# A DiT block on one core: other PSUM banks for the first fc1 groups, the scale rows in one block, the last x tile's transposes one K group earlier

## The chip, the cores and the metric

The kernel runs on one core of one Trainium2 chip. The time is the device time of one execution in microseconds. The compared times are medians of several executions of the same program; the profile is that of one more execution, which has a time of its own. Lower is better.

## What is computed

One diffusion transformer block on x of 2 x 256 tokens with D = 1152, in bfloat16. Cut to what matters here:

```python
mod = (silu(c) @ w_mod).reshape(B, 6, 1, D)
shift_a, scale_a, gate_a, shift_m, scale_m, gate_m = [mod[:, i] for i in range(6)]
h = layernorm(x) * (1 + scale_a) + shift_a
q, k, v = split(h @ wqkv)                    # 2 heads of 576
a = softmax(q @ k.T * 576 ** -0.5) @ v @ wo
x = x + gate_a * a
h2 = layernorm(x) * (1 + scale_m) + shift_m
return x + gate_m * (gelu(h2 @ w_fc1) @ w_fc2)   # F = 4608
```

All weights (some 50 MB) come from device memory once and pass through the core's on-chip memory.

## The kernel before, in words

**Order of the work.** Nothing loops on the chip: the Python code lists every instruction and a small planner (`Sched`) fixes its place on its engine. TensorE (PE) and the DMA queue of SyncE (SP) keep the order in which the code names the work. For VectorE (DVE), ScalarE (ACT) and GpSimd (POOL) the planner picks, by a table of assumed costs, the ready piece with the longest chain behind it, except that `S.first` (L944) writes the first pieces of DVE and ACT out by hand. Every instruction waits, on its engine, for the semaphores of exactly the instructions and transfers that it depends on; on PSUM the unit of dependence is a whole bank (L258 to L279): PE may not write a bank until all readers of what stood there are done.

**The K stage.** The 512 tokens are four x tiles of 128 tokens, `X[:, t, :]`; tiles 0 and 1 are image b = 0, tiles 2 and 3 are b = 1. Each tile is normalised: tiles 1 and 3 take mean and variance from DVE's `bn_stats` (`ln_stats_dve`, L738), tiles 0 and 2 from two accumulating passes on ACT (`ln_stats_act`, L747); POOL raises the variance to the power -1/2 (L745, L754) and DVE then writes `xn` with one `tensor_scalar` over 1152 columns (L763, pieces `xn_0` to `xn_3`). PE transposes the tile with nine 128-wide matmuls (`xn_T`, L773, recorded at L696); `hk` (L812) multiplies 256 columns by the row of 1 + scale_a and so makes K's operand `HK`, on DVE (L819) or ACT (L817).

K itself is `k_pair(kts, i, b)` (L831): two output groups of 128 columns, each a 256-wide matmul per 128 rows kt of the weights. K's weights come kt by kt. For b = 0 the loop L865 goes over kt = 0 to 4 with four pairs each (eight matmuls a kt), with tile 2's transposes behind kt = 1; of kt = 4 it does two pairs, then come tile 3's transposes (`xn_T(3)`, L870), then the other two pairs. Then `k_pair((0, 2, 1, 4, 3), 0, 1)` begins b = 1, which needs `hk_*_1`, and so tile 3's transposes.

**The scale rows.** The first five groups of 128 columns of 1 + scale_a are made early (`mod_kt`, `sc1a(0, 5)`, L860). Columns of groups 5 to 8 come as rows: `quad_mm` (L801) issues, for one kt, four matmuls of 128 columns into the four 32-column parts of the array, into bank 7. L879 does this for kt = 0 to 5 ("scb_0") behind the first K pair of b = 1, L883 for kt = 6 to 8 ("scb_1") behind `k_pair((0, 2, 1), 1, 1)`. A DVE transpose (L888) and `sc1a_5` (L890) follow, then `hk` for kt = 5 to 8. The weights `WSC` for these columns arrive in three transfers (kt 0 to 2, 3 to 5, 6 to 8: `ld_sc5_0`, `ld_sc5_3`, `ld_sc5_6`, issued at L706), behind those that are needed earlier and ahead of K's weights for kt = 5 to 8. The loads of `WQ` (L897) go to the same memory, so each waits on SP until PE has read that kt of `WSC`.

**The fc1 stage.** `xn2_T(t)` (L1142) transposes a tile of the second layer norm into two banks (7 and 6 for even t, 1 and 0 for odd t: groups 0 to 3 in the first, 4 to 8 in the second), and 9 instructions per tile, on DVE (L1154) and ACT (L1157), carry them to `H2T`. `fc1_tile(f, tok0, ntok)` (L1160) makes one group of 128 hidden columns in the next bank of the list `acc`. The first nine groups are made for tokens 0 to 255 first; tile 3's transposes (L1223) stand two groups ahead of their end. Then L1228 to L1230 put two banks, 0 and 1, ahead of the four in use, and L1231 makes the nine groups for tokens 256 to 511, which need tile 3.

Of the kernel before, what the change touches and what calls it, by code (L numbers as in the profile page):

```python
# [493 lines left out]
ALU = mybir.AluOpType  # L494
ACTF = mybir.ActivationFunctionType
# [5 lines left out]
KT = 9  # L501
# [8 lines left out]
KC = 5  # L510
# [5 lines left out]
def c_mm(n):  # L516
    return max(n / 2.4 + 2.5, 27.0)
# [14 lines left out]
def c_dve_fast(n):  # L532
    return 160.0 + 0.37 * n
# [10 lines left out]
def build_kernel(nc, x, c, wqkv, wo, w_mod, w_fc1, w_fc2, out):  # L544
    S = Sched()
# [4 lines left out]
    with (  # L550
# [4 lines left out]
        def sb(off, nbytes, dt=BF16):  # L555
            assert off % 4 == 0 and off + nbytes <= ARENA_BYTES, (off, nbytes)
            v = arena[:, off // 2:(off + nbytes) // 2]
            if dt == F32:
                v = v.bitcast(F32)
            return v  # L560

        def ps32(bank, c0=0, n=512):
            return psum[:, bank * 512 + c0: bank * 512 + c0 + n]
# [19 lines left out]
        def misc(nbytes):  # L583
            o = mo[0]
            mo[0] += (nbytes + 3) // 4 * 4
            assert mo[0] <= ARENA_BYTES
            return o

        def wmat(o, f):
            return sb(o, KT * f * 2).rearrange("p (k f) -> p k f", k=KT)  # L590

        WSC = wmat(O_A, D)
# [58 lines left out]
        NMR = sb(misc(16), 16, F32)  # L651
# [25 lines left out]
        def dve(cost, fn, reads, writes, name):  # L677
            return S.op("dve", cost, fn, reads=reads, writes=writes, name=name)

        def act(cost, fn, reads, writes, name):  # L680
            return S.op("act", cost, fn, reads=reads, writes=writes, name=name)
# [4 lines left out]
        def copy_on(eng, dst, src, n, psum16, name):  # L686
            if eng == "act":
                act(c_act(n), lambda e: e.activation(out=dst, in_=src, func=ACTF.Copy), [src], [dst], name)  # L688
            else:
                dve(c_dve_psum16(n) if psum16 else c_dve_psum32(n), lambda e: e.tensor_copy(dst, src), [src], [dst], name)  # L690

        def mm(o, l, r, st, sp, **kw):
            S.instr(lambda e: e.matmul(o, lhsT=l, rhs=r, start=st, stop=sp, **kw), reads=[l, r], writes=[o])  # L693
# [44 lines left out]
        def ln_stats_dve(src, chunks, bn_t, mv_t, rstd_t, tag):  # L738
            for ci in range(NCH):
                s, o = chunks[ci], bn_t[:, ci * 6:(ci + 1) * 6]  # L740
                dve(550, lambda e, s=s, o=o: e.bn_stats(out=o, in_=s), [s], [o], "bn_%s_%d" % (tag, ci))  # L741
            dve(210, lambda e: e.bn_aggr(out=mv_t, in_=bn_t), [bn_t], [mv_t], "aggr_" + tag)
            var = mv_t[:, 1:2]
            dve(140, lambda e: e.tensor_scalar(out=var, in0=var, scalar1=EPS, scalar2=None, op0=ALU.add), [var], [var], "veps_" + tag)  # L744
            pool(650, lambda e: e.tensor_tensor(out=rstd_t, in0=var, in1=NHALF, op=ALU.pow), [var, NHALF], [rstd_t], "rstd_" + tag)  # L745

        def ln_stats_act(src, junk, mv_t, msq, rstd_t, tag):  # L747
            mean, var = mv_t[:, 0:1], mv_t[:, 1:2]
            act(1420, lambda e: e.activation(out=junk, in_=src, func=ACTF.Square, scale=D ** -0.5, accum_out=msq), [src], [junk, msq], "sq_" + tag)  # L749
            act(1420, lambda e: e.activation(out=junk, in_=src, func=ACTF.Identity, scale=1.0 / D, accum_out=mean), [src], [junk, mean], "sum_" + tag)  # L750
            dve(170, lambda e: e.scalar_tensor_tensor(out=var, in0=mean, scalar=mean, in1=msq, op0=ALU.mult, op1=ALU.subtract),  # L751
                [mean, msq], [var], "nvar_" + tag)
            dve(150, lambda e: e.tensor_scalar(out=var, in0=var, scalar1=-1.0, scalar2=EPS, op0=ALU.mult, op1=ALU.add), [var], [var], "veps_" + tag)  # L753
            pool(650, lambda e: e.tensor_tensor(out=rstd_t, in0=var, in1=NHALF, op=ALU.pow), [var, NHALF], [rstd_t], "rstd_" + tag)  # L754

        for t in range(4):
            xt, xn, mv, rs = X[:, t, :], XN[:, t, :], MV[:, t, :], RSTD[:, t:t + 1]
            if t % 2 == 1:
                ln_stats_dve(xt, [X[:, t, i * CH:(i + 1) * CH] for i in range(NCH)], BN[:, t, :], mv, rs, "ln1_%d" % t)
            else:  # L760
                ln_stats_act(xt, xn, mv, SUMS[:, t:t + 1], rs, "ln1_%d" % t)
            m = MV[:, t, 0:1]
            dve(c_dve_fast(D), lambda e, xt=xt, xn=xn, m=m, rs=rs: e.tensor_scalar(out=xn, in0=xt, scalar1=m, scalar2=rs,  # L763
                                                                                 op0=ALU.subtract, op1=ALU.mult),
                [xt, m, rs], [xn], "xn_%d" % t)
# [7 lines left out]
        def xn_T(t):  # L773
            b = t // 2
            S.unit("pe", KT * c_mm(128), "xnT_%d" % t)
            for kt in range(KT):
                bank, c0 = xt_ps(b, kt)
                tr(ps16(bank, c0 + (t % 2) * 128, 128), XN[:, t, kt * 128:(kt + 1) * 128], IDENT)
# [19 lines left out]
        def quads(w, g0, g1, q):  # L798
            return w.rearrange("p (g q c) -> p g q c", q=4, c=32)[:, g0:g1, q, :]

        def quad_mm(bank, w, g0, g1, kt):  # L801
            n = 32 * (g1 - g0)
            for q in range(4):
                o = psum[32 * q:32 * q + 2, bank * 512:bank * 512 + n].rearrange("p (g c) -> p g c", c=32)
                mm(o, ST[:, kt:18:9], quads(w, g0, g1, q), kt == 0, kt == KT - 1, tile_position=(0, 32 * q))
# [16 lines left out]
        def k_mm(kts, j, b, bank, half):  # L822

            for kt in kts:
                mm(ps32(bank, half * 256, 256), WK[:, kt, j * 128:(j + 1) * 128], HK[:, kt, b * 256:(b + 1) * 256], kt == 0 and half == 0,
                   kt == KT - 1, skip_group_check=True)
# [4 lines left out]
        def k_pair(kts, i, b, bank=None):  # L831
            S.unit("pe", 2 * len(kts) * c_mm(256), "k%d_%d_%d" % (b, i, kts[0]))
            bank = KB[b][i] if bank is None else bank
            if kts[0] == 0:
                for kt in kts:
                    for half in range(2):
                        k_mm((kt,), 2 * i + half, b, bank, half)
            else:
                for half in range(2):
                    k_mm(kts, 2 * i + half, b, bank, half)  # L840
            if kts[-1] == KT - 1:
                eng = "act" if ev_rr[0] % 2 == 0 else "dve"
                ev_rr[0] += 1
                copy_on(eng, QK[:, 9 + 2 * i:11 + 2 * i, b * 256:(b + 1) * 256], ps32(bank).rearrange("p (j t) -> p j t", j=2), 512, False,
                        "k_ev%d_%d" % (b, i))
# [17 lines left out]
        xn_T_copy(0, (8,), "act")  # L863
        xn_T_copy(0, (5, 6, 7), "act")
        for kt in range(KC):  # L865
            for i in range(2 if kt == KC - 1 else 4):
                k_pair((kt,), i, 0)
            if kt == 1:
                xn_T(2)
        xn_T(3)  # L870
        k_pair((KC - 1,), 2, 0)
        k_pair((KC - 1,), 3, 0)
        xn_T_copy(1, (8,), "act")
        xn_T_copy(1, (5, 7), "act")
        xn_T_copy(1, (6,), "dve")
        for kt in range(KC):
            hk(kt, 1, "act" if kt % 2 else "dve")
        k_pair((0, 2, 1, 4, 3), 0, 1)
        S.unit("pe", 6 * 4 * 27.0, "scb_0")  # L879
        for kt in range(6):  # L880
            quad_mm(7, WSC[:, kt, :], KC, KT, kt)
        k_pair((0, 2, 1), 1, 1)
        S.unit("pe", 3 * 4 * 27.0, "scb_1")  # L883
        for kt in range(6, KT):
            quad_mm(7, WSC[:, kt, :], KC, KT, kt)
        n = 32 * (KT - KC)
        sct, scr = ps32(7, 0, n), MT[:, 0:n]
# [42 lines left out]
        for kt in range(KT):  # L930
            for b in range(2):
# [5 lines left out]
                else:  # L937
# [5 lines left out]

        S.first = {  # L944
# [5 lines left out]
        }  # L950

# [160 lines left out]
        acc = [2, 3, 4, 5]  # L1112
# [113 lines left out]
        dma(WFC2[:, 27:36, :], wfc2_v[:, 27:36, :], 9 * P * D * 2, "ld_wfc2_3", run=2304)  # L1226
        mlp_gate(last_h2T[0])
        k = acc_rr[0] % 4  # L1228
        acc[:] = [0, 1] + acc[k:] + acc[:k]
        acc_rr[0] = 0  # L1230
        for f in range(F0):  # L1231
            fc1_tile(f, 256, 256)
# [79 lines left out]
```

## Time and profile before

| | before |
|---|---|
| median of 3 executions | 244.43 us (244.30 to 244.53) |
| the profiled execution | 244.33 us |
| its span, first to last instruction | 242.6 us |
| mean granted TensorE clock | 1.0 |

The span is 1.7 us shorter than the profiled execution's time; the rest lies ahead of the first and behind the last instruction. In the views, a timeline row gives start, length, engine, line, operation, operands and count, and in brackets how long the engine had been idle and what ended that. PE is the matmul, PEld the load of the stationary operand, which runs beside the matmul before; SPq is a DMA being issued. The length of a matmul covers its way through the array, so that matmuls overlap: the step from start to start is what counts. A row of DMA issues ends with the time from issue to landing.

### The profile page before, as it was taken

The numbers are of one execution on the slowest core, as the hardware profiler recorded it, in microseconds if no ns is written. First come the engines' busy times: TensorE is split into PE (matmuls) and PEld (weight loads), VectorE is DVE, ScalarE is ACT, GpSimd is POOL, SyncE is SP. The second block draws the span as 40 slices with busy tenths as digits, with TensorE's granted clock in tenths as the row PEclk, the third lists the DMA queues.
The fourth block names the chain that finished last, engine by engine and source line by source line (L and its number), as shares of the span: only waits on it lengthen the run. The fifth ranks groups of instructions, "written<-read, shape, count | busy, mean of one in ns | idle before, by whom it ended". The sixth has DMA issues, their size and how long they took to land.

```text
span 242.6 us, 3964 instructions
## 1 busy us (share of the span) xinstructions
PE 237.5 (98%) x1700; PEld 145.0 (60%) x1700; DVE 116.2 (48%) x227; ACT 67.0 (28%) x138; POOL 22.4 (9%) x40
## 2 busy tenths in 40 slices
PE   7899999999999999999999999999999999999995
PEld 2588844466657656888644444444566566566564
DVE  2663447988983599669999600000022222111112
ACT  4820340436424206973233322222000000000000
POOL 1300000000023186400000110000000000000000
PEclk9999999999999999999999999999999999999999
DMA  6999999999996999969953499100000000000000
GB/s 220 378 372 390 391 387 385 404 415 406 389 353 195 357 393 392 392 188 399 351 165 83 163 317 369 44 0 3 0 16 19 16 16 16 19 16 16 21 28 19
DMA packets 30299, 51.58 MB, mean 213 GB/s; under 512 B 1611, under 2 KB 16971, under 8 KB 30283
## 3 DMA queue, kind: packets, MB, share of 16 engines
q1 hardware_dynamic: 29600, 50.14, 57.7%
q0 software_dynamic: 512, 1.19, 1.5%
q8 instruction: 13, 0.21, 0.4%
q10 hardware_dynamic: 171, 0.01, 0.0%
q14 instruction: 3, 0.02, 0.0%
HBM read 50.15 MB, written 1.19 MB: 212 GB/s over the span
## 4 chain that ended last, share of the span: by engine, by line
PE 95%; DMA 2%; ACT 1%; DVE 1%; issue 0%
PE psum L693 93%; PE psum L696 2%; DMA arena<-in_x_dram 2%; ACT arena L750 1%; ACT arena L749 0%; DVE arena L763 0%; DVE arena L819 0%; DVE arena L1254 0%; DVE arena L1255 0%; DVE arena L751 0%; DVE arena L809 0%; DVE arena L753 0%; ACT arena L733 0%
## 5 line engine op out<-in xcount | busy, mean ns | idle before, releaser
L693 PE MATMUL psum<-arena 128*128 128x384 bf16 (+8 forms) x1611 | 234.1, 314 | 2.2 <-POOL arena L719 1.5
L693 PEld LDWEIGHTS psum<-arena 128*128 128x128 bf16 (+2 forms) x1611 | 139.7, 97 | 92.2 <-issue 3.6
L1254 DVE TENSOR_TENSOR arena<-psum,arena 128x384 f32<-128x384 f32 (+2 forms) x13 | 6.8, 526 | 88.8 <-PE psum L693 88.8
L1167 ACT ACTIVATE arena<-psum 128x512 bf16<-128x512 f32 (+1 forms) x45 | 22.8, 511 | 42.4 <-PE psum L693 42.4
L688 ACT ACTIVATE arena<-psum 128x512 bf16<-128x512 f32 (+6 forms) x37 | 18.7, 534 | 36.2 <-PE psum L693 35.9
L1067 DVE SCALAR_TENSOR_TENSOR arena<-arena 128x1152 f32<-128x1152 bf16 x16 | 21.3, 1411 | 0.0
L1038 DVE SCALAR_TENSOR_TENSOR arena<-arena 128x896 f32<-128x896 bf16 x16 | 17.7, 1142 | 0.0
L690 DVE CAST arena<-psum 128x512 bf16<-128x512 f32 (+1 forms) x12 | 7.7, 646 | 10.0 <-PE psum L693 9.9
L674 POOL DMA_DIRECT2D dit_scratch<-arena x6 | 3.6, 605 | 92.9 <-ACT arena L688 53.6
L1133 POOL TENSOR_TENSOR arena<-arena 128x384 f32<-128x384 f32 x12 | 10.9, 911 | 10.7 <-DVE arena L1132 8.8
L741 DVE BATCH_NORM_STATS2 arena<-arena 128x6 f32<-128x384 f32 (+1 forms) x18 | 9.5, 549 | 4.2 <-DMA arena<-in_x_dram 3.5
L1138 ACT ACTIVATE arena<-arena 128x1152 bf16<-128x1152 f32 x4 | 5.4, 1344 | 9.7 <-DVE arena L1137 9.7
L1132 DVE TENSOR_TENSOR arena<-psum,arena 128x384 f32<-128x384 f32 x12 | 6.5, 546 | 2.8 <-DMA arena<-dit_scratch 2.0
L696 PE MATMUL psum<-arena 128*128 128x128 bf16 (+1 forms) x89 | 7.1, 219 | 0.4 <-DMA arena<-in_c_dram 0.3
L696 PEld LDWEIGHTS psum<-arena 128*128 128x128 bf16 (+1 forms) x89 | 5.8, 98 | 2.8 <-DMA arena<-in_c_dram 1.2
L1255 DVE TENSOR_TENSOR arena<-arena 128x384 bf16<-128x384 f32 (+2 forms) x13 | 6.9, 527 | 0.5
L1157 ACT ACTIVATE arena<-psum,arena 128x128 bf16<-128x128 bf16 x16 | 6.1, 455 | 2.9 <-PE psum L696 2.1
L1154 DVE TENSOR_SCALAR arena<-psum,arena 128x128 bf16<-128x128 bf16 x20 | 5.5, 335 | 2.9 <-PE psum L696 2.9
L982 ACT ACTIVATE arena<-psum,arena 128x256 bf16<-128x256 f32 x8 | 3.7, 469 | 0.4 <-DVE arena L979 0.3
L745 POOL TENSOR_TENSOR arena<-arena 128x1 f32<-128x1 f32 x6 | 3.3, 553 | 4.9 <-DVE arena L744 4.9
L935 ACT ACTIVATE arena<-arena 128x256 bf16<-128x256 bf16 x6 | 2.5, 495 | 3.3 <-DVE arena L929 3.3
L978 DVE TENSOR_REDUCE arena<-psum 128x2 f32<-128x512 f32 x4 | 2.7, 687 | 0.9 <-PE psum L693 0.9
(57 smaller groups left out, 52.5 us busy)
## 6 DMA issues: line engine op xcount, KB each, us to landing
arena<-in_w_fc_dram SPq DMA_DIRECT2D x9, 1152.0 KB, 6.9
arena<-in_w_fc_dram SPq DMA_DIRECT2D x4, 2592.0 KB, 18.2
arena<-in_w_mod_dram SPq DMA_DIRECT2D x3, 1920.0 KB, 19.6
arena<-in_wqkv_dram SPq DMA_DIRECT2D x18, 288.0 KB, 10.5
arena<-in_w_mod_dram SPq DMA_DIRECT2D x3, 864.0 KB, 13.2
arena<-in_wqkv_dram SPq DMA_DIRECT2D x1, 2592.0 KB, 16.7
arena<-in_wo_dram SPq DMA_DIRECT2D x1, 2592.0 KB, 26.1
arena<-in_w_mod_dram SPq DMA_DIRECT2D x1, 2592.0 KB, 17.6
```

Of the source, the lines that this page charges most:

```text
L688: act(c_act(n), lambda e: e.activation(out=dst, in_=src, func=ACTF.Copy), [src], [dst], name)
L690: dve(c_dve_psum16(n) if psum16 else c_dve_psum32(n), lambda e: e.tensor_copy(dst, src), [src], [dst], name)
L693: S.instr(lambda e: e.matmul(o, lhsT=l, rhs=r, start=st, stop=sp, **kw), reads=[l, r], writes=[o])
L696: S.instr(lambda e: e.transpose(o, i_, idn), reads=[i_, idn], writes=[o])
L741: dve(550, lambda e, s=s, o=o: e.bn_stats(out=o, in_=s), [s], [o], "bn_%s_%d" % (tag, ci))
L1038: dve(150 + FG * 1.1, lambda e, o=o, w=w, s1=s1: e.scalar_tensor_tensor(out=o, in0=w, scalar=s1, in1=o, op0=ALU.mult, op1=ALU.add), [w, s1 ...
L1067: u = dve(1300, lambda e, o=o, w=w, s1=s1: e.scalar_tensor_tensor(out=o, in0=w, scalar=s1, in1=o, op0=ALU.mult, op1=ALU.add), [w, s1, o], ...
L1132: dve(550, lambda e, o=o, ga=ga, x1c=x1c: e.tensor_tensor(out=x1c, in0=o, in1=ga, op=ALU.mult), [o, ga], [x1c], "wo_t1_%d_%d" % (t, ci))
L1133: S.op("pool", 930, lambda e, xs=xs, x1c=x1c: e.tensor_tensor(out=x1c, in0=x1c, in1=xs, op=ALU.add), reads=[x1c, xs], writes=[x1c], name=" ...
L1167: act(c_act(ntok), lambda e: e.activation(out=dst, in_=o, func=ACTF.Gelu_apprx_tanh), [o], [dst], "gelu_%d_%d" % (f, tok0))
L1254: dve(c_dve_psum32(w), lambda e, o=o, gm=gm, t1=t1: e.tensor_tensor(out=t1, in0=o, in1=gm, op=ALU.mult), [o, gm], [t1], "fc2_t1_%d_%d" % ( ...
L1255: dve(c_dve_32(w), lambda e, t1=t1, x1c=x1c, ost=ost: e.tensor_tensor(out=ost, in0=t1, in1=x1c, op=ALU.add), [t1, x1c], [ost], "fc2_out_%d ...
```

## The change

1. Tile 2 is normalised on ACT: DVE makes `-mean * rstd` in one small instruction (`nmr_2`), ACT writes `xn_2` with one activation over 1152 columns. In the orders written by hand `nmr_2` stands ahead of `sc1a_0` on DVE, `xn_2` leaves DVE's list and stands ahead of `hk_4_0` on ACT.
2. Of kt = 4 one pair instead of two goes ahead of tile 3's transposes, three instead of two behind.
3. The scale rows of kt = 0 to 8 are one block, where kt = 6 to 8 stood.
4. The first two of the fc1 groups for tokens 256 to 511 use banks 6 and 7 instead of 0 and 1.

```diff
             m = MV[:, t, 0:1]
+            if t == 2:
+                nm = NMR[:, t:t + 1]
+                dve(170, lambda e, nm=nm, m=m, rs=rs: e.scalar_tensor_tensor(out=nm, in0=m, scalar=-1.0, in1=rs, op0=ALU.mult, op1=ALU.mult),
+                    [m, rs], [nm], "nmr_%d" % t)
+                act(1344, lambda e, xt=xt, xn=xn, nm=nm, rs=rs: e.activation(out=xn, in_=xt, func=ACTF.Identity, scale=rs, bias=nm),
+                    [xt, rs, nm], [xn], "xn_%d" % t)
+                continue
...
         for kt in range(KC):
-            for i in range(2 if kt == KC - 1 else 4):
+            for i in range(1 if kt == KC - 1 else 4):
                 k_pair((kt,), i, 0)
             if kt == 1:
                 xn_T(2)
         xn_T(3)
-        k_pair((KC - 1,), 2, 0)
-        k_pair((KC - 1,), 3, 0)
+        for i in range(1, 4):
+            k_pair((KC - 1,), i, 0)
...
         k_pair((0, 2, 1, 4, 3), 0, 1)
-        S.unit("pe", 6 * 4 * 27.0, "scb_0")
-        for kt in range(6):
-            quad_mm(7, WSC[:, kt, :], KC, KT, kt)
         k_pair((0, 2, 1), 1, 1)
-        S.unit("pe", 3 * 4 * 27.0, "scb_1")
-        for kt in range(6, KT):
+        S.unit("pe", KT * 4 * 27.0, "scb")
+        for kt in range(KT):
             quad_mm(7, WSC[:, kt, :], KC, KT, kt)
...
-                    "xn_1", "xn_0", "nvar_ln1_2", "veps_ln1_2", "xnT_cp0_0", "sc1a_0", "hk_0_0", "hk_1_0", "hk_2_0", "hk_3_0", "xn_2",
+                    "xn_1", "xn_0", "nvar_ln1_2", "veps_ln1_2", "xnT_cp0_0", "nmr_2", "sc1a_0", "hk_0_0", "hk_1_0", "hk_2_0", "hk_3_0",
...
-            "act": ["touch", "ld_c", "sq_ln1_0", "c_tanh", "sum_ln1_0", "sq_ln1_2", "sum_ln1_2", "xnT_cp0_8", "xnT_cp0_5", "hk_4_0",
+            "act": ["touch", "ld_c", "sq_ln1_0", "c_tanh", "sum_ln1_0", "sq_ln1_2", "sum_ln1_2", "xnT_cp0_8", "xnT_cp0_5", "xn_2", "hk_4_0",
...
-        acc[:] = [0, 1] + acc[k:] + acc[:k]
+        acc[:] = [6, 7] + acc[k:] + acc[:k]
```

## Prediction

> **What bounds the kernel now.** The page first: how busy is the busiest engine, and does anything other than its own work set the end?
>
> ```profile
> PE 237.5 (98%) x1700; PEld 145.0 (60%) x1700; DVE 116.2 (48%) x227; ACT 67.0 (28%) x138; POOL 22.4 (9%) x40
> ```
>
> PE is busy for 237.5 us, 98% of the span. Its busy time hides short stalls, because a matmul's recorded length covers its way through the array. So the second view is the timeline of PE and PEld in the two places that the change touches, where I compare starts with counts. First the K stage, from tile 2's transposes (L696) to the end of the scale rows (128*2):
>
> ```profile
> 13.32 0.67 PE L696 MATMUL psum<-arena 128*128 128x128 bf16 x9
> 13.83 2.35 PE L693 MATMUL psum<-arena 128*128 128x256 bf16 x20
> 16.01 0.67 PE L696 MATMUL psum<-arena 128*128 128x128 bf16 x9
> 16.51 0.60 PE L693 MATMUL psum<-arena 128*128 128x256 bf16 x4
> ...
> 17.12 1.03 PEld L693 LDWEIGHTS psum<-arena 128*128 128x128 bf16 x10 [0.29 <-DVE arena L819]
> 18.36 0.08 PEld L693 LDWEIGHTS psum<-arena 128*2 128x2 bf16 x1 [0.21 <-issue]
> 18.79 0.10 PEld L693 LDWEIGHTS psum<-arena 128*128 128x128 bf16 x1
> 19.55 0.10 PEld L693 LDWEIGHTS psum<-arena 128*2 128x2 bf16 x8 [0.21 <-DMA arena<-in_w_mod_dram]
> 19.82 0.10 PEld L693 LDWEIGHTS psum<-arena 128*128 128x128 bf16 x1
> ```
>
> Twenty 256-wide matmuls take 13.83 to 16.01: 0.109 us a step. Nine 128-wide ones take 13.32 to 13.83: 0.056. With these two steps every stall can be found:
>
> - Four matmuls from 16.51 are done at 16.95; the next starts at 17.12, released by DVE's `hk` (L819). Lost: **0.17**.
> - Ten from 17.12 should be done at 18.21; the scale rows start at 18.36. Lost: 0.15.
> - Four column parts run side by side, so a kt of scale rows costs one 128-wide step. Six kt from 18.36 end at 18.70, and K goes on at 18.79: 0.09. Six matmuls from 18.79 end at 19.45, the second block starts at 19.55: 0.10. Its three kt end at 19.72, K goes on at 19.82: 0.10. So to enter a block costs 0.10 and to leave it 0.09, and the 0.15 above is 0.10 for entering plus 0.05 for late `hk` pieces.
>
> Then the fc1 stage, from the last two groups of the first 256 tokens to the first group of the others, with the readers of tile 3's (106.43, 107.12) and of tile 2's (104.58) transposes:
>
> ```profile
> 106.22 2.46 PE L693 MATMUL psum<-arena 128*128 128x256 bf16 x19
> 108.39 0.10 PEld L693 LDWEIGHTS psum<-arena 128*128 128x128 bf16 x1 [0.32 <-DVE arena L1154]
> 106.43 1.60 DVE L1154 TENSOR_SCALAR arena<-psum,arena 128x128 bf16<-128x128 bf16 x6 [1.85 <-PE psum L696]
> 107.12 1.16 ACT L1157 ACTIVATE arena<-psum,arena 128x128 bf16<-128x128 bf16 x3 [0.81 <-PE psum L693]
> 104.58 0.81 ACT L1157 ACTIVATE arena<-psum,arena 128x128 bf16<-128x128 bf16 x2
> ```
>
> And the last long piece of the chain of work that ended last (start, length, what):
>
> ```profile
> 108.42 131.75 PE psum L693 x792
> ```
>
> The first row's nineteenth matmul is the first of the other tokens; its weights load at 108.39 and it starts at 108.42, where the chain picks up. Eighteen from 106.22 are done at 108.18. Lost: **0.23**. The view names DVE, but its six were done at 108.03; ACT's three end at 108.28, and they read bank 0, which the next group writes.
>
> **The change, part by part.** Own time of the profiled execution: 244.33.
>
> *Tile 2 on ACT.* The rows of the other engines:
>
> ```profile
> 9.65 0.22 DVE L751 SCALAR_TENSOR_TENSOR arena<-arena 128x1 f32<-128x1 f32 x1 [0.52 <-ACT arena L750]
> 9.90 1.09 ACT L688 ACTIVATE arena<-psum 128x256 bf16<-128x256 bf16 x2 [0.29 <-PE psum L696]
> 10.13 0.55 POOL L754 TENSOR_TENSOR arena<-arena 128x1 f32<-128x1 f32 x1 [1.61 <-DVE arena L753]
> 11.02 0.17 DVE L809 TENSOR_SCALAR arena<-psum 128x10 f32<-128x10 f32 x1 [0.77 <-PE psum L693]
> 12.20 0.57 DVE L763 TENSOR_SCALAR arena<-arena 128x1152 bf16<-128x1152 bf16 x1
> 12.69 1.47 DVE L741 BATCH_NORM_STATS2 arena<-arena 128x6 f32<-128x384 bf16 x3
> 15.28 0.58 DVE L763 TENSOR_SCALAR arena<-arena 128x1152 bf16<-128x1152 bf16 x1 [0.66 <-POOL arena L745]
> 16.71 0.87 DVE L819 TENSOR_SCALAR arena<-psum,arena 128x256 bf16<-128x256 bf16 x3 [0.85 <-PE psum L696]
> ...
> L1137 DVE SCALAR_TENSOR_TENSOR arena<-arena x4: 159/354/769, 89.7 to 101.8; 128x1 f32<-128x1 f32 x4
> ...
> L1138 ACT ACTIVATE arena<-arena 128x1152 bf16<-128x1152 f32 x4 | 5.4, 1344 | 9.7 <-DVE arena L1137 9.7
> ...
> 4.70 0.59 SPq L674 DMA_DIRECT2D arena<-in_x_dram  x1
> arena<-in_x_dram SPq DMA_DIRECT2D x1, 288.0 KB, 7.6
> ```
>
> `nmr_2` waits for POOL until 10.68 (10.13 + 0.55). Behind it on DVE stands `sc1a_0`, which PE releases at 11.02 anyway. The same instruction in the second layer norm (L1137) took 0.16 to 0.77, its like just ahead on DVE (L751) 0.22. With 0.22 it hides in DVE's idle 0.77; with 0.77 it ends at 11.45, `sc1a_0` is 0.43 late, and with it every `hk` and K's start. I take the 0.22, the row that is nearest in time: cost nothing. (At the long end PE would reach kt = 6 of the scale rows, below, at 19.13 + 0.43 = 19.56, as before: that stage would gain nothing, 244.20.) `xn_2` starts on ACT at about 11.0, when `xnT_cp0_5` ends (9.90 + 1.09), and takes 1.34 by the same operation on f32 (L1138): done by 12.4. PE wants it at 13.32. Behind it `hk_4_0` starts at 12.4 instead of right behind `sc1a_0` (11.02 + 0.17); PE first needs it for kt = 4, two matmuls ahead of 15.79, at 15.57. Both hide, the first with 0.9 to spare. DVE's `bn_stats` of tile 3 no longer waits for `xn_2` (12.20), but for its data: 4.70 + 7.6 = 12.3. It starts 0.38 earlier, and `xn_3` ends at 15.48 instead of 15.86.
>
> *Tile 3's transposes two matmuls earlier.* They start at 16.01 - 0.22 = 15.79, with `xn_3` 0.3 ahead. The `hk` pieces of b = 1 start at 16.49 instead of 16.71, and could release K at 16.90, while PE with six matmuls behind the transposes is busy until 16.95. The 0.17 goes; the next `hk` pieces come 0.22 earlier too and PE only 0.17, so the 0.05 goes as well. Gain so far: 0.22. The cover is thin (0.05), but what comes next makes that unimportant.
>
> *One block of scale rows.* One entry and one exit less: 0.10 + 0.09 = 0.19. So PE would get to the rows at 16.95 + 10 x 0.109 + 6 x 0.109 + 0.10 = 18.79, and to kt = 6 six steps later, at **19.13**, where before it got there at 19.55. Here a wait appears that before was hidden. The transfers of these weights, each issue with its time to landing, and the queue in the 0.3 us from 15.2:
>
> ```profile
> arena<-in_w_mod_dram SPq DMA_DIRECT2D x1, 384.0 KB, 8.6
> ...
> 7.71 0.53 SPq L674 DMA_DIRECT2D arena<-in_w_mod_dram  x1
> arena<-in_w_mod_dram SPq DMA_DIRECT2D x1, 384.0 KB, 10.6
> ...
> 8.28 1.30 SPq L674 DMA_DIRECT2D arena<-in_w_mod_dram  x1
> arena<-in_w_mod_dram SPq DMA_DIRECT2D x1, 384.0 KB, 11.1
> ...
> q8 instruction: 1, 0.02, 23.8%
> ...
> 14.91 2.59 SPq L674 DMA_DIRECT2D arena<-in_w_mod_dram  x1
> arena<-in_w_mod_dram SPq DMA_DIRECT2D x1, 864.0 KB, 14.3
> ```
>
> `ld_sc5_3` lands at 7.71 + 10.6 = 18.3, in time for kt = 3. `ld_sc5_6` lands at 8.28 + 11.1 = **19.4**. Before, PE asked for it 0.15 later than that; now 0.27 earlier, and PE stands. Its issue time depends on nothing that the change moves. Everything behind the rows on PE waits with them, so of the 0.41 no more than 19.55 - 19.4 = 0.15 is kept. From this go a semaphore's way and the refilling of PE's queue: nothing, if the twelve matmuls behind the wait keep 0.056 a kt; at worst they go singly, like the tiny matmuls of `mod_kt`:
>
> ```profile
> 8.68 0.54 PE L693 MATMUL psum<-arena 128*128 128x2 bf16 x15
> ```
>
> Fifteen in 0.54 are 0.036 each, twelve 0.43 instead of 0.17. So this stage gains between 0.15 and 0.15 - 0.26 = -0.11 while the wait binds, and up to 0.41 if it doesn't. The nearest row is the second block of before: eight loads within 0.10 just after the landing, no single file. I take **0.07**. The Trainium skill, page "TensorE: Matmul & The Clock Gate", section "Wait — 56ns, not 53.3ns?", says that starts are never closer than about 25 ns; by that the twelve take at least 0.30, and the sum would be 0.13 worse. The trace speaks against it here: eight loads of 0.08 start within 0.02.
>
> SP's queue: the `WQ` loads wait for these rows and are issued some 0.4 later. At 19.1 the last load ahead of them still needs until 14.91 + 14.3 = 29.2, so the DMA engines don't run dry: nothing.
>
> *Banks 6 and 7.* Their last readers were tile 2's, done at 105.39. The first new group then needs only its operands, kt by kt: DVE's are done at 108.03, and kt = 8 is wanted at 108.18 + 8 x 0.109 = 109.05 against ACT's 108.28. Gain **0.23**; nothing is late next, as the chain from 108.42 on is PE's own work alone for 131.75 us.
>
> Sum: 0.07 + 0.23 = **0.30**; 244.33 - 0.30 = 244.03 for that execution. The median shown is 0.10 higher, so I predict **244.13**. 0.2% is 0.49 us, about what a measurement of this kernel can tell from no change.
>
> **The rivals.**
>
> *A: the wait doesn't bind.* Three equal transfers in a row take 8.6, 10.6 and 11.1 from issue to landing: the first step, 2.0, is out of line with the second, 0.5. Just ahead of the second's landing falls one packet of instructions (q8), which holds one DMA engine for 23.8% of 16 x 0.3 = 1.14 us. With two steps of 0.5 `ld_sc5_6` would land at 8.28 + 9.6 = 17.9. If that packet falls elsewhere, or the transfers run 0.3 faster, all 0.41 is kept: 0.64, 243.79. Against it: PE's order and DMA's are unchanged until then. The Trainium skill, page "Runtime: NRT & Kernel Launch", section "Instruction fetch mechanics", has crossing a block of instructions cost one step of a DMA tail, mostly hidden; by that rule, this rival. The landings disagree.
>
> *B: only the banks.* Twelve matmuls in single file, or a landing 0.2 later: the stage gains -0.11 to 0, the sum is 0.12 to 0.23, 244.20 to 244.31.
>
> *C, slower: DVE's order in the attention stage.* The planner's assumed times shift, so a gate sum (L1038) may be put ahead of a softmax piece there.
>
> ```profile
> L1038 DVE SCALAR_TENSOR_TENSOR arena<-arena 128x896 f32<-128x896 bf16 x16 | 17.7, 1142 | 0.0
> ...
> 62.46 0.68 DVE L986 TENSOR_TENSOR arena<-arena 128x512 bf16<-128x512 bf16 x1
> ...
> 63.77 0.39 PE L696 MATMUL psum<-arena 128*128 128x128 bf16 x4
> ```
>
> The last softmax piece ends at 63.14, its transposes start at 63.77: 0.63 of cover. One sum ahead of it costs 1.14 - 0.63 = 0.51 and leaves +0.21; two cost 1.65, +1.35, 245.78. It decides from a delay of 0.93 on. Against it: both would have to fall ahead of the same last piece.
>
> **How the numbers follow.** Forecast 0.60, A 0.18, B 0.14, C 0.08. The likeliest one's own range is 243.95 to 244.20. The range for 8 in 10 takes in A and B, and no gain at all, each with the 0.1 by which the executions shown differ: **243.70 to 244.55**; C is left out. Faster by over 0.49 (under 243.94): A and a tail of the forecast, 0.20. Slower (over 244.92): C with two, 0.06. Within: 0.74.
>
> **What would show it.** In the timeline of after: no wait for L819 near 17; one block of 128*2 loads from 18.8, with a wait for in_w_mod inside it until about 19.45, and K going on near 19.75 (before 19.82), or near 19.4 by A, with no such wait. The first group of the other tokens right behind the second last (0.109 apart), with no wait for L1154. `sc1a_0` still at 11.02: later, and `nmr_2` was mis-sized. The prediction is wrong if `ld_sc5_6` lands before 19.1 or after 19.6, or if PE shows a wait between 20 and 108.

## The result, and the profile after

| | before | after |
|---|---|---|
| median | 244.50 us (244.30 to 244.75, 17 executions) | 243.98 us (243.90 to 244.29, 17 executions) |
| ratio to before, 95% interval | | 0.9982 [0.9975, 0.9988] |
| the profiled execution | 244.33 us, span 242.6 | 243.94 us, span 242.2 |

The ratio says 0.44 us less, with 0.29 to 0.61 as its interval: faster, but by only about 0.2%, at most 0.25%; the two medians themselves differ by 0.52. Predicted were 0.30 less and 244.13. The granted clock was 1.0 in both profiles.

The page of the changed kernel, its span and its first part:

```profile
span 242.2 us, 3963 instructions
PE 236.9 (98%) x1700; PEld 145.1 (60%) x1700; DVE 116.0 (48%) x227; ACT 68.2 (28%) x139; POOL 22.4 (9%) x40
```

PE is still the bound. ACT has one instruction more, `xn_2`; DVE keeps its number, since `nmr_2` came for `xn_2`.

The K stage of the changed kernel in the timeline. `nmr_2` is now L765, `xn_2` L767, `sc1a_0` L816, `hk` L826 on DVE, the transpose of the scale rows L892 and `sc1a_5` L894:

```profile
10.71 0.16 DVE L765 SCALAR_TENSOR_TENSOR arena<-arena 128x1 f32<-128x1 f32 x1 [0.46 <-POOL arena L754]
10.91 1.35 ACT L767 ACTIVATE arena<-arena 128x1152 bf16<-128x1152 bf16 x1
11.02 0.17 DVE L816 TENSOR_SCALAR arena<-psum 128x10 f32<-128x10 f32 x1
...
12.34 1.48 DVE L741 BATCH_NORM_STATS2 arena<-arena 128x6 f32<-128x384 bf16 x3
...
14.95 0.58 DVE L770 TENSOR_SCALAR arena<-arena 128x1152 bf16<-128x1152 bf16 x1 [0.66 <-POOL arena L745]
...
15.79 0.67 PE L696 MATMUL psum<-arena 128*128 128x128 bf16 x9
16.24 2.34 PEld L693 LDWEIGHTS psum<-arena 128*128 128x128 bf16 x22
...
18.79 2.03 PEld L693 LDWEIGHTS psum<-arena 128*2 128x2 bf16 x50 [0.21 <-issue]
20.25 0.32 DVE L892 STREAM_TRANSPOSE arena<-psum 128x128 f32<-128x128 f32 x1 [2.68 <-PE psum L693]
...
20.81 1.46 DVE L826 TENSOR_SCALAR arena<-arena 128x256 bf16<-128x256 bf16 x7
21.15 0.88 PEld L693 LDWEIGHTS psum<-arena 128*128 128x128 bf16 x9 [0.33 <-DVE arena L826]
```

Tile 3's transposes start at 15.79 and the rows at 18.79, both as forecast, with no wait near 17: 22 weight loads follow one another. Inside the block there is no wait for a transfer either, where the prediction had one until 19.45, and K goes on at 19.40, where the prediction had 19.75 and its rival A 19.4. Instead a new wait stands at 21.15, behind the block: PE wants the first `hk` of b = 1 for kt = 5 (`hk_5_0`, 20.81), which comes behind the rows' transpose at 20.25. From PE's starts (one at 20.83, the next at 21.15, where a step is 0.109) the loss is **0.21**.

The same place of before, rows that the prediction did not use:

```profile
19.55 2.46 PEld L693 LDWEIGHTS psum<-arena 128*2 128x2 bf16 x33 [0.21 <-DMA arena<-in_w_mod_dram]
20.19 0.32 DVE L888 STREAM_TRANSPOSE arena<-psum 128x128 f32<-128x128 f32 x1 [2.41 <-PE psum L693]
```

Before, the last of the 36 row matmuls started at 19.68 and the transpose came 0.51 later. After, the last one started at 19.25, 0.43 earlier, but the transpose came 1.00 later, at 20.25: no earlier than before, although PE was done earlier. That needs a cause.

The transfer that the prediction feared, `ld_sc5_6`, in the timeline (its issue) and the view of DMA issues of the changed kernel:

```profile
8.14 1.44 SPq L674 DMA_DIRECT2D arena<-in_w_mod_dram  x1
```

```profile
arena<-in_w_mod_dram SPq DMA_DIRECT2D x1, 384.0 KB, 10.4
```

It landed at 8.14 + 10.4 = 18.5 (18.58 in the trace's records), not at 19.4, and kt = 6 is wanted at 18.79 + 6 x 0.056 = 19.13.

The fc1 stage in the timeline, and pieces of the chain that ended last:

```profile
106.02 5.18 PE L693 MATMUL psum<-arena 128*128 128x256 bf16 x46
106.22 1.60 DVE L1158 TENSOR_SCALAR arena<-psum,arena 128x128 bf16<-128x128 bf16 x6 [1.85 <-PE psum L696]
106.92 1.15 ACT L1161 ACTIVATE arena<-psum,arena 128x128 bf16<-128x128 bf16 x3 [0.81 <-PE psum L693]
```

```profile
20.26 0.32 DVE arena L892
...
20.81 0.30 DVE arena L826
21.11 0.05 issue
21.15 37.52 PE psum L693 x267
...
106.18 133.56 PE psum L693 x810
```

The gap near 108 is gone: 46 matmuls run through from 106.02, past the end of tile 3's readers, and the chain's last piece has 810 matmuls where before it had 792 from 108.42 on; the eighteen that it gained are those ahead of the old gap. But the chain now leaves PE at 20.26 for the rows' transpose and `hk`.

Where the 0.44 came from, in the profiles: 0.22 from the K stage up to the rows, 0.19 from one block less (entering and leaving, some 0.095 each, are paid once), 0.23 from the banks, and -0.21 for the new wait: 0.43, where the two profiled executions differ by 0.39.

### The profile page after: what moved, and what is told of

Its sections match the earlier page's. It is cut to its first block, busy times and chain, and to the rows that moved or that the text cites. A ratio compares the mean times of both kernels' runs of the same rounds, so it can differ in the third digit from the quotient of the medians.

```text
span 242.2 us, 3963 instructions
## 1 busy us (share of the span) xinstructions
PE 236.9 (98%) x1700; PEld 145.1 (60%) x1700; DVE 116.0 (48%) x227; ACT 68.2 (28%) x139; POOL 22.4 (9%) x40
## 4 chain that ended last, share of the span: by engine, by line
PE 95%; DMA 2%; DVE 1%; ACT 1%; issue 0%
PE psum L693 93%; PE psum L696 2%; DMA arena<-in_x_dram 2%; ACT arena L750 1%; ACT arena L749 0%; DVE arena L826 0%; DVE arena L770 0%; DVE arena L892 0%; DVE arena L1258 0%; DVE arena L1259 0%; DVE arena L751 0%; DVE arena L894 0%; DVE arena L816 0%; DVE arena L753 0%; ACT arena L733 0%
```

## The experiments

**Theories.** Why does the transpose come a whole us after the last row matmul?

- *Counting.* Every matmul, when it completes, raises PE's semaphore, the counter that the readers of its results wait on, by one. In the trace's semaphore records the 36 of the block are counted 0.034 us apart, from 19.03 to 20.22, while PE starts four of them per 0.056, 0.014 each. Before, the 24 of the first block had been counted by 19.38, ahead of the second block, whose twelve were counted from 19.79 to 20.17. So merging the blocks puts 36 counts, 36 x 0.034 = 1.2 us, in one row ahead of the transpose. Rival to it: the results themselves are that late.
- *Landing*, the prediction's: PE stands in the block for `ld_sc5_6`, and the profile of after caught a lucky execution.

**The parts alone.** Each time the rest of the change is undone.

`e1_banks_only`:

```diff
-        acc[:] = [0, 1] + acc[k:] + acc[:k]
+        acc[:] = [6, 7] + acc[k:] + acc[:k]
```

> Only the banks 6 and 7 for the first two fc1 groups of the other tokens; all else as before. Both theories of the K stage say the same here: the first group starts right behind the one before it, the 0.23 us that PE stood at 108.2 are gone, nothing comes in their place: 0.23 us less than before (ratio 0.9991), and the K stage as before, K going on at 19.82.

Measured: 244.28 against 244.43, 0.9991 [0.9980, 1.0003]; profiled 244.18. The medians differ by 0.15 and the interval holds the expected 0.23 and no gain alike; the timeline decides: the gap near 108 is gone, and the K stage has its old stalls (0.17 for `hk` behind tile 3's transposes, two blocks).

`e2_transposes_only` (parts 1 and 2: tile 2 on ACT, tile 3's transposes earlier; the lines of part 1 are those of the change):

```diff
...
-            for i in range(2 if kt == KC - 1 else 4):
+            for i in range(1 if kt == KC - 1 else 4):
...
-        k_pair((KC - 1,), 2, 0)
-        k_pair((KC - 1,), 3, 0)
+        for i in range(1, 4):
+            k_pair((KC - 1,), i, 0)
```

> Tile 2 on ACT and tile 3's transposes two matmuls earlier, with two blocks of scale rows and banks 0 and 1 as before. Counting theory (each matmul's completion is counted on PE's semaphore one at a time, 0.034 us apart, so that DVE learns late that the scale rows are done): the second block, 12 matmuls, starts at 19.33 instead of 19.55, its last count comes 0.22 earlier too, no wait behind it, 0.22 us less than before (0.9991). Landing theory (ld_sc5_6 at 19.4 as in the profile of before): PE waits for it inside the second block, 0.1 to 0.15 us less than before.

Measured: 244.23, 0.9984 [0.9968, 1.0001]; profiled 244.45. PE's weight loads and the transpose (here L895) in its timeline:

```profile
18.20 0.15 PEld L693 LDWEIGHTS psum<-arena 128*2 128x2 bf16 x12 [0.21 <-issue]
18.55 0.82 PEld L693 LDWEIGHTS psum<-arena 128*2 128x2 bf16 x18 [0.19 <-DMA arena<-in_w_mod_dram]
19.67 2.35 PEld L693 LDWEIGHTS psum<-arena 128*2 128x2 bf16 x32 [0.30 <-DMA arena<-in_w_mod_dram]
20.30 0.32 DVE L895 STREAM_TRANSPOSE arena<-psum 128x128 f32<-128x128 f32 x1 [2.67 <-PE psum L693]
```

Here PE does stand for the rows' weights, twice: 0.17 at 18.3 and some 0.09 more than entering costs at 19.4. In this execution `ld_sc5_3` landed at 18.50 and `ld_sc5_6` at 19.62. So the landing theory describes something real; it just isn't what the profile of after shows.

`e3_block_only` (part 3):

```diff
         k_pair((0, 2, 1, 4, 3), 0, 1)
-        S.unit("pe", 6 * 4 * 27.0, "scb_0")
-        for kt in range(6):
-            quad_mm(7, WSC[:, kt, :], KC, KT, kt)
         k_pair((0, 2, 1), 1, 1)
-        S.unit("pe", 3 * 4 * 27.0, "scb_1")
-        for kt in range(6, KT):
+        S.unit("pe", KT * 4 * 27.0, "scb")
+        for kt in range(KT):
             quad_mm(7, WSC[:, kt, :], KC, KT, kt)
```

> One block of scale rows at the place of the second, all else as before. Counting theory: the block starts at 19.01, its 36 counts at 0.034 end at about 20.45, scb_T starts there and K's kt = 5 waits for hk_5_0 until about 21.37, where PE could be there at 21.14: a wait of 0.23 us that takes the 0.19 of the saved block back, time as before (0.9998 to 1.0002). Landing theory: kt = 6 wanted at 19.35, no wait for counts, 0.1 to 0.19 us less than before (0.9992 to 0.9996) and scb_T about 0.5 us behind the last row.

Measured: 244.51 against 244.43, 0.9994 [0.9977, 1.0012]: the median is 0.08 higher, the ratio says 0.15 lower, and the interval holds no change. In its timeline:

```profile
19.25 2.03 PEld L693 LDWEIGHTS psum<-arena 128*2 128x2 bf16 x50 [0.21 <-issue]
20.71 0.32 DVE L885 STREAM_TRANSPOSE arena<-psum 128x128 f32<-128x128 f32 x1 [2.69 <-PE psum L693]
...
21.61 0.44 PEld L693 LDWEIGHTS psum<-arena 128*128 128x128 bf16 x5 [0.33 <-DVE arena L819]
```

From block to transpose it is 1.46 again, as in after (18.79 to 20.25), and the same 0.21 is lost behind it. By itself the one block gives 0.19 and takes 0.21: nothing. PE waits for none of the rows' transfers here. (The block starts at 19.25 and not at the expected 19.01, because K started 0.13 later than in the profile of before and tile 3's transposes another 0.10 late; x's tile 3 landed at 12.98.)

**The suspected cost taken away.** `e4_count_block_once` is the changed kernel with one count for the block: only its last matmul raises the semaphore, and the transpose waits for that. Work, order and operands stay.

```diff
+                if u.name == "scb":
+                    for ins in u.instrs[:-1]:
+                        ins.quiet = True
...
-                    else:
+                    elif not ins.quiet:
                         bi.then_inc(sems[e], 1)
```

> The changed kernel, but of the 36 matmuls of the scale rows only the last adds to PE's semaphore. Counting theory: scb_T starts about 0.3 us behind the start of the last row matmul, near 19.55 instead of 20.25, the wait for hk_5_0 (0.21 us) is gone, 0.21 us less than the changed kernel, 0.65 less than before (0.9973). If scb_T was late for another reason (landing, DVE's own order, the transpose itself): as the changed kernel, 0.44 less than before (0.9982), scb_T still near 20.25.

Measured: 243.78 (243.62 to 244.18, 12 executions) against 244.43, 0.9969 [0.9958, 0.9981]; profiled 243.62, span 241.9. In its timeline:

```profile
18.73 3.34 PEld L703 LDWEIGHTS psum<-arena 128*2 128x2 bf16 x62 [0.21 <-issue]
19.46 0.32 DVE L902 STREAM_TRANSPOSE arena<-psum 128x128 f32<-128x128 f32 x1 [1.96 <-PE psum L703]
```

From block to transpose 0.73 instead of 1.46, and the loads run through: no wait behind the block. Nothing but the counting was changed, and measured from the block's start the reader begins 0.73 earlier, so it is the counting that had made it late. This settles counting against its rival. (The block also starts 0.06 earlier here than in the profile of after; with the 0.21 that is 0.27 of the 0.32 between the two profiled times.) The medians of after and of this differ by 0.20; the intervals of their ratios overlap a little, so the size of the step rests on the 0.21 of the timeline.

`e5_count_small_once` gives also each group of five tiny matmuls of `mod_kt` one count:

```diff
-                if u.name == "scb":
+                if u.name == "scb" or u.name.startswith("sca_"):
```

> The changed kernel, with one count for the 36 matmuls of the scale rows and one for each five tiny matmuls of mod_kt ahead of sc1a_0. Counting theory: the tiny matmuls run 0.027 apart but are counted 0.034 apart, so sc1a_0 (11.02, 0.38 behind the start of the last of them) comes about 0.12 earlier, K starts near 11.45 instead of 11.57, and the wait for hk_5_0 is gone as in the run with one count: 0.21 + 0.12 = 0.33 less than the changed kernel, 0.77 less than before (0.9969 or a little under, about 243.65). Landing theory: K earlier by 0.12 only asks earlier for ld_sc5_6, which landed between 18.5 and 19.6 in the profiles so far; with kt = 6 wanted near 19.0 most executions wait for it and the 0.12 is lost in them: 243.8.

Measured: 243.89 (243.55 to 244.22, 7 executions), 0.9977 [0.9966, 0.9987]: no better than one count for the block, and not the expected 243.65. Its timeline, of an execution of 243.96, tells part of why:

```profile
11.57 1.92 PE L703 MATMUL psum<-arena 128*128 128x256 bf16 x16 [0.35 <-DVE arena L836]
12.68 1.48 DVE L751 BATCH_NORM_STATS2 arena<-arena 128x6 f32<-128x384 bf16 x3 [0.39 <-DMA arena<-in_x_dram]
...
15.92 0.51 PEld L706 LDWEIGHTS psum<-arena 128*128 128x128 bf16 x9 [0.24 <-DVE arena L780]
```

The wait ahead of K is 0.35 where after has 0.52 in the view's bracket, 0.17 less. But K starts at 11.57, no earlier than in after, because the last tiny matmul started at 10.82 here and at 10.64 there. Tile 3 of x landed at 12.66 in this execution, DVE's `bn_stats` waits for it, and PE gives 0.12 back ahead of tile 3's transposes; it loses another 0.12 at 96.1, where a piece of the second layer norm is late. What the other executions lost is not shown.

**The block moved.** In `e6_block_early` the block stands six matmuls earlier, so that PE asks for kt = 6 sooner:

```diff
-        k_pair((0, 2, 1), 1, 1)
         S.unit("pe", KT * 4 * 27.0, "scb")
         for kt in range(KT):
             quad_mm(7, WSC[:, kt, :], KC, KT, kt)
+        k_pair((0, 2, 1), 1, 1)
```

> The changed kernel with the one block ahead of k_pair((0, 2, 1), 1, 1) instead of behind it, every matmul counted. kt = 6 is wanted at about 18.47. Counting theory alone: counts end near 19.4 to 19.6, hk_5_0 long before K's kt = 5, the 0.21 wait gone: 0.21 less than the changed kernel (243.77). Landing theory: PE stands in the block until the landing, 18.5 at the earliest and 19.6 at the latest in the profiles so far: a wait of 0.05 to 1.1 us with in_w_mod as its releaser, the time between 243.85 and 244.9, scattered by execution more than any other kernel's.

Measured: 244.29 (243.94 to 245.12), 0.9994 [0.9985, 1.0004]; profiled 244.70. In its timeline:

```profile
18.03 0.15 PEld L693 LDWEIGHTS psum<-arena 128*2 128x2 bf16 x12 [0.21 <-issue]
18.35 0.15 PEld L693 LDWEIGHTS psum<-arena 128*2 128x2 bf16 x12 [0.17 <-DMA arena<-in_w_mod_dram]
19.49 1.59 PEld L693 LDWEIGHTS psum<-arena 128*2 128x2 bf16 x25 [0.98 <-DMA arena<-in_w_mod_dram]
20.12 0.32 DVE L892 STREAM_TRANSPOSE arena<-psum 128x128 f32<-128x128 f32 x1 [2.66 <-PE psum L693]
```

The landings bind here, `ld_sc5_3` with about 0.15 and `ld_sc5_6` with 0.98, and the wait for `hk_5_0` is gone: six more matmuls stand between the block and K's kt = 5, and the first 24 counts ran off while PE stood, so the transpose comes 0.63 after the last twelve begin. The executions spread over 1.2 us, and the profiled one is among the late ones.

`e7_count_once_block_later` is `e5_count_small_once` with the block two matmuls later; `e9_block_four_later` is `e4_count_block_once` with it four matmuls later (the edit of e9; in e7 only kt = 4 moves):

```diff
-        k_pair((0, 2, 1), 1, 1)
+        k_pair((0, 2, 1, 4, 3), 1, 1)
...
-        k_pair((4, 3), 1, 1)
```

> As the run with one count for scale rows and tiny matmuls, and the block two matmuls later (0.22 us). kt = 6 is wanted near 19.2, twelve matmuls (1.31 us) are left behind the block for the chain to hk_5_0, which takes about 1.2 from the last row matmul. Counting theory: no wait, same time as without the move (243.65). Landing theory: fewer executions wait for ld_sc5_6, less scatter and a median up to 0.1 lower than without the move.

> One count for the 36 matmuls of the scale rows, and the block behind k_pair((4, 3), 1, 1) too, four matmuls (0.44 us) later than in the changed kernel. kt = 6 is wanted near 19.55 (K starting at 11.57); ten matmuls are left behind the block, from the last row matmul to K's kt = 5 some 1.24 us, against 1.17 that the chain from there to hk_5_0 took in the run with one count. Counting theory: no wait behind the block, the median of the run with one count (243.78) or a little under. Landing theory: ld_sc5_6 landed at 19.6 at the latest in ten profiles, so almost no execution waits in the block, and the ones some 0.25 above the others are gone: 243.6 to 243.8, less scatter.

Measured: e7 243.89 (243.55 to 244.37), 0.9975 [0.9964, 0.9985], with 0.23 lost ahead of tile 3's transposes, x's tile 3 having landed at 12.74. e9 243.79 (243.63 to 244.10), 0.9972 [0.9961, 0.9982], profiled 243.77. In e9's timeline:

```profile
19.30 4.76 PEld L703 LDWEIGHTS psum<-arena 128*2 128x2 bf16 x75 [0.21 <-issue]
20.03 0.32 DVE L902 STREAM_TRANSPOSE arena<-psum 128x128 f32<-128x128 f32 x1 [2.40 <-PE psum L703]
```

No wait from the rows on, with kt = 6 asked for at 19.64, later than every landing of `ld_sc5_6` seen with this order of the loads. The median is that of e4, which suggests that in e4 too the landing seldom bound.

`e10_rows_land_later` is the changed kernel with K's weights for kt = 5 issued ahead of `ld_sc5_6` instead of behind it:

```diff
+                if k0 == 6:
+                    dma(WK[:, KC, :], wqkv_v[:, KC, D:2 * D], P * D * 2, "ld_wk%d" % KC, run=2304)
...
+                if kt == KC:
+                    continue
```

> The changed kernel, with K's weights of kt = 5 issued ahead of ld_sc5_6, so that the latter lands 0.75 us later: near 19.35 where the instruction packet comes after 15.6, near 20.2 where it comes before 15.5. Counting theory alone: same time as the changed kernel in every execution (243.98), PE waits for hk_5_0 only. Both together: in executions with the late packet PE stands 0.2 to 0.3 in the block with in_w_mod as releaser and then no more than 0.05 for hk_5_0, since the counts of the first 24 still go on meanwhile: about 244.0; with the early packet it stands about 1.1 in the block: about 244.85. So a median near the changed kernel's and a second group some 0.8 higher.

Measured: 244.38 (244.04 to 245.20), 0.9994 [0.9986, 1.0003]; profiled 245.20, its slowest execution. There the rows' last transfer landed at 20.59. The expectation had 19.35 for an instruction packet that starts after 15.6; the packet started at 15.75, so the rule that the expectation used failed here. Two groups of times do not show either: the twelve executions are spread from 244.04 to 244.78, with the one at 245.20 apart. In its timeline:

```profile
18.94 0.32 PEld L693 LDWEIGHTS psum<-arena 128*2 128x2 bf16 x24 [0.21 <-issue]
20.64 1.37 PEld L693 LDWEIGHTS psum<-arena 128*2 128x2 bf16 x23 [1.37 <-DMA arena<-in_w_mod_dram]
21.27 0.32 DVE L896 STREAM_TRANSPOSE arena<-psum 128x128 f32<-128x128 f32 x1 [3.56 <-PE psum L693]
```

PE waits 1.37 inside the block and not at all behind it. So the landing is a second limit beside the count: whichever ends later sets the end of this stage.

**Part 1 taken back.** `e8_tile2_on_dve` is the changed kernel with `xn_2` on DVE, as before (the orders written by hand are those of before, too):

```diff
-            if t == 2:
+            if t == 9:
...
```

> The changed kernel with tile 2 normalised on DVE as before, in its old place in DVE's list. By the prediction's working tile 3's xn ends at 15.86 instead of 15.48, its transposes are wanted at 15.79 and wait until about 15.92 or 16.0; the hk pieces and everything behind come 0.15 to 0.22 later; counting theory: the wait for hk_5_0 behind the block stays 0.21, as it is counted from the block, so the time is 0.15 to 0.22 more than the changed kernel (244.15). Landing theory: the block's wait swallows it, same time as the changed kernel.

Measured: 244.15 (244.06 to 244.34), 0.9987 [0.9979, 0.9996]; profiled 244.10. In its timeline:

```profile
15.97 0.51 PEld L696 LDWEIGHTS psum<-arena 128*128 128x128 bf16 x9 [0.24 <-DVE arena L770]
...
21.34 0.66 PEld L693 LDWEIGHTS psum<-arena 128*128 128x128 bf16 x7 [0.33 <-DVE arena L826]
```

Tile 3's transposes wait 0.13 for `xn_3`, and the wait behind the block stays. DVE's `bn_stats` of tile 3 started at 12.74 here, behind `xn_2`; but x's tile 3 landed at 12.66 in this execution, so most of that wait would have come with `xn_2` on ACT too, as in `e5_count_small_once`. With a landing at 12.3 the 12.74 would be DVE's doing alone. By that estimate the part is worth up to 0.13 in an execution, when tile 3 lands early; the medians of this kernel and of after differ by 0.17, with intervals that overlap.

**The changed kernel once more, and one mend.** `a2_changed_again` is after without an edit. `e11_tile3_lands_earlier` is `e9_block_four_later` with x's tile 3 issued ahead of K's weights for kt = 1:

```diff
-                if kt == 1:
+                if kt == 0:
```

> The changed kernel once more, unaltered, for a second profile beside the two others on the same chip. Both theories: 243.98. If the instruction packet comes before 15.5 in this profile: ld_sc5_6 lands at 19.4 to 19.6, PE stands 0.3 to 0.5 inside the block and less than 0.1 for hk_5_0, and the execution takes 244.05 to 244.25; if after 15.6: no wait in the block, 0.21 for hk_5_0, 243.9 to 244.0.

> The run with one count and the block four matmuls later, and tile 3's x issued ahead of ld_wk1 instead of behind it, so that it lands 0.75 us earlier (11.6 to 12.4 instead of 12.3 to 13.1), and ld_wk1 0.75 later (near 12.3; wanted at K's start + 0.87, 12.44). If tile 3's landing is what makes some executions 0.1 to 0.5 longer (bn_stats started at its landing in every profile of the changed kernel and its variants with tile 2 on ACT): no wait ahead of tile 3's transposes, the upper executions go, median 243.65 to 243.75. If the landing has no part in it: 243.79 with the same scatter. If ld_wk1 binds: PE waits for it behind kt = 0, up to 0.3 us more.

Measured: a2 244.16 (243.86 to 244.54, 11 executions), 0.9984 [0.9976, 0.9993]; profiled 244.54, its slowest, not the 243.9 to 244.0 that was expected of it. In that execution:

```profile
13.17 1.48 DVE L741 BATCH_NORM_STATS2 arena<-arena 128x6 f32<-128x384 bf16 x3 [0.59 <-DMA arena<-in_x_dram]
...
16.40 0.51 PEld L696 LDWEIGHTS psum<-arena 128*128 128x128 bf16 x9 [0.44 <-DVE arena L770]
...
21.77 0.22 PEld L693 LDWEIGHTS psum<-arena 128*128 128x128 bf16 x3 [0.33 <-DVE arena L826]
```

K started at 11.86, 0.29 later than in the first profile, x's tile 3 landed at 13.14 and PE lost 0.33 for it: 0.62 together, against 0.60 between the two profiled times. The wait behind the block is the same to a hundredth. So late executions of this kernel need not be those in which `ld_sc5_6` is late.

e11: 243.79 (243.70 to 244.01, 12 executions), 0.9965 [0.9949, 0.9982]: the median that e9 has, where 243.65 to 243.75 was expected. PE's weight loads in its profile, taken of its slowest execution (244.01):

```profile
11.60 0.77 PEld L703 LDWEIGHTS psum<-arena 128*128 128x128 bf16 x8 [0.82 <-DVE arena L836]
...
12.74 0.78 PEld L703 LDWEIGHTS psum<-arena 128*128 128x128 bf16 x8 [0.37 <-DVE arena L836]
```

Tile 3 now lands at 11.88 and its transposes wait for nothing, but K's weights for kt = 1, put behind it, land at 12.63, and PE waits 0.28 for those eight matmuls. (The bracket names `hk`, yet DVE's were done at 12.3; the landing is the later one.) The wait moved from one transfer to the next. That this execution was the slowest fits; the other executions have no trace.

## Why the prediction was right, and where it was wrong

The size came out nearly: 0.30 forecast, 0.44 measured with 0.29 to 0.61, and 244.13 is 0.15 above the median of after. By its steps:

- *Tile 2 on ACT costs nothing*: right. `nmr_2` took 0.16, forecast 0.22; `sc1a_0` started at 11.02 as before. `xn_3` started at 14.95 and so ended at 15.53, forecast 15.48.
- *Tile 3's transposes at 15.79, 0.22 gained*: right to a hundredth, but the cover ("0.3 ahead") hangs on the landing of x's tile 3. That landed between 12.2 and 13.1 in the profiles that keep its place in the queue, a margin that the prediction took from one execution.
- *One block less, 0.19*: right. Entering and leaving cost 0.09 to 0.10 each wherever no landing fell between.
- *"Everything behind the rows on PE waits with them ... I take 0.07"*: the step that failed. It priced a wait for `ld_sc5_6` inside the block. In the profile of after that transfer landed at 18.58 and PE waited for nothing there. What took part of the gain back is the wait for `hk_5_0` behind the block, 0.21, so that stage kept 0.41 - 0.21 = 0.20 and not 0.07. The low bound of that term, -0.11, was misread as well: the 0.54 of the fifteen tiny matmuls includes the last one's way through the array, their starts are 0.027 apart and not 0.036, so twelve in single file would have taken 0.32 and left 0.00. The cause is one that the prediction did not name: it checked who reads the rows' weights, and not when the rows' reader is released. The view was there: before's transpose started 0.51 after the last of 36 short matmuls.
- *Rival A* had the landing right (it wanted 17.9 or any time before 19.13) and gave 243.79; the median is 0.19 above that, about the 0.21 of the wait that it did not have either. With the count taken away, e4 comes to 243.78.
- *Rival A's reason*, that one packet of instructions moves the landing, has support, and one profile against it. In the three profiles where that packet started at 15.25 to 15.40 (before, e2, e6) `ld_sc5_6` landed at 19.41 to 19.62; in the ten others that leave the order of the rows' loads alone the packet started at 15.56 to 16.7 and it landed at 18.51 to 18.98. But in e10 the packet started at 15.75, and `ld_sc5_3`, which stands ahead of the edit in the queue, still landed 2.66 behind `ld_sc5_0`, as in the three early profiles (2.48 to 2.65); in the ten others the distance is 1.07 to 1.11, and e8 is among them, whose packet started at the same 15.75. So the packet's start alone doesn't tell late landings from early ones. No run moved the packet by itself, and the reason stays open. The Trainium skill, page "Runtime: NRT & Kernel Launch", section "Instruction fetch mechanics", calls such a crossing mostly hidden; in e6, with the early packet, PE stood 0.98.
- *Rival B* did not come in the profile of after: the 36 row matmuls started within 0.46, not in single file, and `ld_sc5_6` landed earlier than forecast, not later.
- *Banks, 0.23*: right. The gap is gone in after, and 0.23 remains in e2 and e3, which keep the old banks.
- *Rival C*: it did not come. In the attention stage of after's timeline

```profile
62.26 0.68 DVE L990 TENSOR_TENSOR arena<-arena 128x512 bf16<-128x512 bf16 x1
...
63.56 0.39 PE L696 MATMUL psum<-arena 128*128 128x128 bf16 x4
```

  the last softmax piece ends at 62.94 and its transposes start at 63.56: the cover of 0.62 is that of before.
- *Wrong if `ld_sc5_6` lands before 19.1, or if PE shows a wait between 20 and 108*: by both of its own signs the prediction's mechanism for this stage was wrong, with a landing at 18.58 and a wait at 21.15. That the total was close is in part luck, because two errors cancelled in part: a wait that was not there (0.34 taken off) and one that was not seen (0.21).

What stays open: how much of the spread of after (twelve of its first 17 executions within 243.90 to 244.04, five from 244.14 to 244.29) comes from `ld_sc5_6` and how much from x's tile 3. What makes `ld_sc5_6` late in some executions is open too. No profile of after itself caught a late landing of it; the one late execution that was seen was late by x's tile 3 and a late start of K.

## What to carry to other kernels

Before many short matmuls are gathered into one block, look at when their reader is released and not only at when PE is through: the count of completions can be the slower of the two, and one count at the end of the block, where nobody waits for the others, removes it. A step that is moved ahead of a hidden wait needs its margins read from several executions, since a transfer's landing moved here by about 1 us from one to the next. By the timelines, of the four parts the banks and the earlier transposes (which tile 2 on ACT makes room for) paid; the one block paid only with the single count (about 243.8 instead of 244.0).

## What the runs showed of the hardware

- PE's semaphore was raised no more often than once per 0.034 us in these traces: 36 matmuls of a block, started 0.013 apart on average, took 1.2 us to be counted, and their reader came 1.46 after the block's start instead of 0.73 with one count.
- Matmuls in the four column parts are not held to one start per 25 ns, the distance that the Trainium skill gives (page "TensorE: Matmul & The Clock Gate", section "Wait — 56ns, not 53.3ns?"): in e6 twelve weight loads of this kind begin and end within 0.15 us, and in after 36 matmuls start within 0.46.
- A switch between whole-array matmuls and column parts cost PE 0.09 to 0.10 each way.
- One transfer with the same place in the queue landed up to 1.1 us apart in executions of kernels that keep the order of the rows' loads (`ld_sc5_6`: issued at 7.86 to 8.63, landed at 18.51 to 19.62).
